# Global rows copied by VectorE alone, a planner that counts GpSimd's eight transfers, and a new order of loads, in a sliding-window attention followed by a two-layer MLP

## The chip, the cores and the metric

The kernel runs on one core of a Trainium2 chip. The metric is the device time in microseconds (us) of one execution; smaller is better. The kernel before took 221.41 us (median of 3 runs, 220.68 to 222.15). Each execution also reports the span of the core (from its first to its last instruction, some 1.8 us shorter than the time) and the mean granted clock of TensorE, where 1.0 is full speed. A run is called slow when it is over 1.5% above the fastest run of the same kernel.

## The reference, cut to what matters

```python
# q, k, v: [4 batches, 8 heads, 768 positions, 64], float32;  w_in: [512, 2048], w_out: [2048, 512]
rel = pos[:, None] - pos[None, :]
is_global = pos[None, :] < 8
is_local = (rel >= 0) & (rel < 96)
keep = is_global | is_local
scores = q @ k.T / 8 - slope[head] * dist          # dist = rel inside the window, 96 for global keys
a = softmax(where(keep, scores, -1e9))
x = (a @ v) with the heads side by side            # [3072, 512]
h = x @ w_in
out = (h - tanh(h)) @ w_out                        # [3072, 512]
```

A query tile of 128 positions needs the keys of its own tile, the last 96 positions of the tile before, and the first eight (global) positions of its batch. There are 24 tiles, numbered 0 to 23, six to a batch.

## The kernel before

The program is planned while it is being built. Every piece of work is an entry with an engine (or a choice of engines), an assumed duration, what it must come after, and the buffers that it takes and gives back. A greedy planner puts the entries in order of time, and each engine then executes its entries strictly in that order. So a wrong assumption of the planner changes no result, but it can put a piece of work behind something that waits.

For tile `u`: GpSimd issues the loads of k, q and v, which also cast float32 to bfloat16. TensorE transposes q and k (`T`; from tile `PE_T` on, a DMA transpose does it). TensorE makes scores with the own tile and with the tile before (`S`), ScalarE the exponentials (`E`), VectorE the masks (`M`), TensorE the product with v (`AV`), VectorE the division (`R`). The result is transposed into `xT` (`X` on TensorE, or a DMA transpose). Then come 16 slices of the first projection (`m1`), `h - tanh(h)` on ScalarE and VectorE, and the second projection (`m2`).

Keys of the previous tile that lie outside the window leave room, so the global keys and values are copied into its first eight rows:

```python
    def a_K(u, e):
        (nc.gpsimd if e is POOL else nc.vector).tensor_copy(out=qk[u][:, 1, :, 0:G], in_=qk[u - u % NQ][:, 1, :, 0:G])

    def a_V(u, e):
        (nc.gpsimd if e is POOL else nc.vector).tensor_copy(
            out=vb[u % NV][0:G, :, 0:Dh], in_=vb[(u - u % NQ) % NV][0:G, :, 0:Dh]
        )
    ...
        if 1 <= i < NQ - 1:
            op(("K", u), (DVE, POOL), (0.2, 0.35), lambda e, u=u: a_K(u, e), after=[("S", u, 0)])
            op(("V", u), (DVE, POOL), (0.3, 0.7), lambda e, u=u: a_V(u, e), after=[("AV", u)])
        op(("AV", u), PE, 0.5, lambda u=u: a_AV(u),
           after=[(pm, u, 0), (pm, u, 1) if i else None, ("ld", "v", u), ("V", u - 1) if i >= 2 else None],
           take=["big"], give=["p0", "p1"] if i else ["p0"])
```

So `AV` of tile u + 1 waits for the copy `V` of tile u. The planner may give a copy to VectorE or to GpSimd, whichever it thinks is done first. The loads stand in GpSimd's order too:

```python
    before = [
        ("t", 0), ("t", 1), ("t", 2), ("in", 0), ("in", 1), ("in", 2), ("t", 3), ("t", 4), ("in", 3),
        ("out", 0), ("out", 1), ("out", 2), ("out", 3), ("t", 5), ("t", 6), ("t", 7),
    ]
    ...
            op(key, POOL, us, fn, after=[prev and ("issue", prev)] + free_v, take=["kq"] if nm == "k" else [],
               dma=dma, pri=-2)
```

`("t", u)` is the k, q and v of tile u, `("in", j)` and `("out", j)` are quarters of the weights. The built program of before has nine copies on GpSimd: three of V and six of K.

The softmax here doesn't subtract the row's maximum and nothing guards it: scores larger than these inputs give would overflow.

## Time and profile before

| | before (profiled run) |
|---|---|
| time of this run / median of the timed runs | 224.73 / 221.41 us |
| span | 223.0 us |
| TensorE busy | 212.1 us, 95% |
| VectorE, ScalarE, GpSimd busy | 59%, 57%, 32% |
| longest wait of TensorE | 3.6 us, at 60 us |
| mean granted clock | 0.992 |

The profiled run is slow, 1.8% above the fastest. These are lines of the page: busy time by engine, then the span in 40 slices (a digit is the busy share in tenths), and the chain of work that ended last.

```profile
span 223.0 us, 5219 instructions
...
PE 212.1 (95%) x2130; PEld 136.7 (61%) x2130; DVE 130.7 (59%) x265; ACT 126.4 (57%) x206; POOL 70.8 (32%) x94
...
PE   7979999999859999999999999999999999999993
...
DMA  9999999999999627999999999824312111011112
...
PE 74%; DMA 18%; POOL 5%; issue 1%; ACT 0%; DVE 0%; SPq 0%; POOLq 0%
```

TensorE bounds the kernel, and its row has one hole after the start, in slices 11 and 12, near 60 us. The waits of TensorE (who waited for whom: us in total, times, longest) name it:

```profile
engine line waited for: us in total, times, longest us
PE big L235 <- POOL vb_109 L250: 3.6, 1, 3.6
PE one L291 <- DMA w_in_bf_94<-in_moe_w_in_dram: 1.4, 1, 1.4
```

Line 235 is in `a_AV`, line 250 is the V copy of tile 7 into buffer vb_109. GpSimd's own timeline (start, duration, what, and in brackets the idle time before it with its releaser) shows why the copy came late:

```profile
50.75 0.88 POOL L157 DMA_DIRECT2D vb_105<-in_v_dram  x1
...
58.34 0.88 POOL L157 DMA_DIRECT2D kq<-in_k_dram  x1 [0.18 <-PE big L235]
62.40 0.88 POOL L157 DMA_DIRECT2D kq<-in_q_dram  x1 [3.19 <-DMA vb_105<-in_v_dram]
63.27 0.60 POOL L250 COPY vb_109<-vb_108 8x512 bf16<-8x512 bf16 x1
```

The load at 62.40 had to wait for the load of vb_105, which is the eighth before it (50.75 and the seven issues up to 58.34), and the copy that TensorE needed stood behind this load. A table of stretches around the hole (columns: stretch, length, then busy time with count of PE, PEld, DVE, ACT and POOL, the granted clock, a DMA share and GB/s) shows the second part of the loss:

```profile
60.00:62.00 2.00, 0.31 (x3) 0.10 (x2) 0.69 (x1) 0.38 (x1) 0.00 (x0) 1.00 1.93 67
62.00:64.00 2.00, 0.07 (x2) 0.07 (x2) 0.00 (x0) 0.00 (x0) 1.60 (x3) 0.91 1.65 158
64.00:66.00 2.00, 2.00 (x25) 1.38 (x25) 0.00 (x0) 0.51 (x1) 0.64 (x2) 0.50 1.73 217
66.00:68.00 2.00, 2.00 (x8) 0.76 (x7) 1.42 (x3) 1.10 (x2) 0.00 (x0) 0.73 1.61 151
```

After the wait TensorE runs at half its clock until about 67 us.

### The profile page before, as it was taken

The page shows a single profiled execution, that of the slowest core. Times are in us where ns is not written, and L with a number is a line of the kernel's source. Part 1 is how long each engine was busy: PE and PEld are TensorE (multiplying, and loading weights), DVE is VectorE, ACT ScalarE, POOL GpSimd, SP SyncE. Part 2 cuts the span into 40 slices and gives each one's busy share as a digit, 9 for nine tenths or more (in the row PEclk, how much of TensorE's full clock was granted, in tenths as well). Part 3 has the DMA queues.
Part 4 walks back from the last instruction along what each step waited for, and adds up shares of the span by engine and source line. Part 5 has one row for each costly group of instructions (what it writes and reads, how often), then busy time and mean ns, then how long its engine had stood idle before and what let it go on. Part 6 is the DMA issues. An engine that isn't in the chain of part 4 may idle for free.

```text
span 223.0 us, 5219 instructions
## 1 busy us (share of the span) xinstructions
PE 212.1 (95%) x2130; PEld 136.7 (61%) x2130; DVE 130.7 (59%) x265; ACT 126.4 (57%) x206; POOL 70.8 (32%) x94
## 2 busy tenths in 40 slices
PE   7979999999859999999999999999999999999993
PEld 2548977785437858855665656565656555555553
DVE  8545896488504758855786777576755444444300
ACT  5578775676513586653785755765573444544320
POOL 8973634988440009845303930000000000000000
PEclk9999999999979999999999999999999999999999
DMA  9999999999999627999999999824312111011112
GB/s 127 145 198 171 199 214 181 165 176 167 120 167 178 118 78 81 139 126 160 181 182 130 171 138 151 160 41 103 97 20 74 47 47 47 0 50 49 47 47 94
DMA packets 106311, 26.68 MB, mean 120 GB/s; under 512 B 100528, under 2 KB 102832, under 8 KB 106288
## 3 DMA queue, kind: packets, MB, share of 16 engines
q0 software_dynamic: 75488, 13.37, 81.8%
q1 hardware_dynamic: 29760, 12.72, 31.4%
q10 hardware_dynamic: 1040, 0.26, 0.5%
q8 instruction: 16, 0.26, 0.5%
q14 instruction: 7, 0.06, 0.1%
HBM read 27.26 MB, written 6.29 MB: 150 GB/s over the span
## 4 chain that ended last, share of the span: by engine, by line
PE 74%; DMA 18%; POOL 5%; issue 1%; ACT 0%; DVE 0%; SPq 0%; POOLq 0%
PE one L318 33%; PE one L291 31%; DMA vb_105<-in_v_dram 5%; DMA w_in_bf_97<-in_moe_w_in_dram 4%; DMA w_in_bf_95<-in_moe_w_in_dram 4%; DMA qk<-kq 4%; PE big L208 4%; POOL kq L157 2%; PE big L231 2%; PE big L235 2%; PE one L330 2%; PE one L173 0%; POOL vb_102 L157 0%; POOL vb_103 L157 0%; POOL vb_104 L157 0%
## 5 line engine op out<-in xcount | busy, mean ns | idle before, releaser
L302 ACT ACTIVATE th<-one 128x384 f32<-128x384 f32 (+1 forms) x116 | 60.6, 527 | 58.0 <-PE one L291 56.9
L308 DVE TENSOR_TENSOR g<-one,th 128x384 bf16<-128x384 f32 (+1 forms) x116 | 68.5, 597 | 41.6 <-ACT th L302 38.9
L318 PEld LDWEIGHTS <-g 128*128 128x128 bf16 x368 | 33.7, 98 | 33.0 <-issue 1.3
L216 ACT ACTIVATE pd<-big 128x1024 bf16<-128x1024 f32 x24 | 24.5, 1022 | 8.0 <-PE big L208 7.8
L291 PE MATMUL one<-xT,w_in_bf_94 128*128 128x128 bf16 (+1 forms) x224 | 25.4, 258 | 1.4 <-DMA w_in_bf_94<-in_moe_w_in_dram 1.4
L291 PE MATMUL one<-xT,w_in_bf_95 128*128 128x128 bf16 (+1 forms) x224 | 25.3, 257 | 0.4 <-DMA w_in_bf_95<-in_moe_w_in_dram 0.4
L291 PE MATMUL one<-xT,w_in_bf_97 128*128 128x128 bf16 (+1 forms) x224 | 25.3, 257 | 0.1
L291 PE MATMUL one<-xT,w_in_bf_96 128*128 128x128 bf16 (+1 forms) x224 | 25.1, 257 | 0.0
L318 PE MATMUL one<-w_out_bf_101,g 128*128 128x512 bf16 x92 | 24.5, 390 | 0.0
L216 ACT ACTIVATE po<-big 128x1024 bf16<-128x1024 f32 x20 | 20.5, 1026 | 5.7 <-PE big L208 5.7
L157 POOL DMA_DIRECT2D kq<-in_q_dram x23 | 20.7, 901 | 9.3 <-DMA vb_105<-in_v_dram 3.2
L318 PE MATMUL one<-w_out_bf_100,g 128*128 128x512 bf16 x92 | 23.7, 380 | 0.0
L318 PE MATMUL one<-w_out_bf_98,g 128*128 128x512 bf16 x92 | 23.7, 380 | 0.0
L318 PE MATMUL one<-w_out_bf_99,g 128*128 128x512 bf16 x92 | 23.6, 379 | 0.0
L157 POOL DMA_DIRECT2D kq<-in_k_dram x23 | 20.6, 897 | 7.2 <-DMA kq<-in_q_dram 2.5
L291 PEld LDWEIGHTS <-w_in_bf_94 128*128 128x128 bf16 x224 | 17.6, 114 | 7.7 <-DMA w_in_bf_94<-in_moe_w_in_dram 1.5
L291 PEld LDWEIGHTS <-w_in_bf_96 128*128 128x128 bf16 x224 | 17.6, 114 | 5.7
L291 PEld LDWEIGHTS <-w_in_bf_97 128*128 128x128 bf16 x224 | 17.5, 114 | 5.9 <-DMA w_in_bf_97<-in_moe_w_in_dram 0.3
L346 ACT COPY ot<-one 128x512 f32<-128x512 f32 x23 | 13.5, 588 | 12.8 <-PE one L318 12.8
L291 PEld LDWEIGHTS <-w_in_bf_95 128*128 128x128 bf16 x224 | 17.3, 113 | 5.6 <-DMA w_in_bf_95<-in_moe_w_in_dram 0.7
L220 DVE TENSOR_TENSOR pd<-pd,mk 128x1024 bf16<-128x1024 bf16 x21 | 14.5, 690 | 7.4 <-ACT pd L216 7.3
L220 DVE TENSOR_TENSOR po<-po,mk 128x1024 bf16<-128x1024 bf16 x18 | 12.4, 691 | 10.2 <-ACT po L216 10.2
(104 smaller groups left out, 198.0 us busy)
## 6 DMA issues: line engine op xcount, KB each, us to landing
out_dram<-ot SPq DMA_DIRECT2D x23, 256.0 KB, 2.5
kq<-in_k_dram POOLq DMA_DIRECT2D x23, 128.0 KB, 10.8
kq<-in_q_dram POOLq DMA_DIRECT2D x23, 128.0 KB, 11.1
w_in_bf_94<-in_moe_w_in_dram POOLq DMA_DIRECT2D x1, 512.0 KB, 7.5
w_in_bf_95<-in_moe_w_in_dram POOLq DMA_DIRECT2D x1, 512.0 KB, 9.5
w_in_bf_96<-in_moe_w_in_dram POOLq DMA_DIRECT2D x1, 512.0 KB, 11.1
w_in_bf_97<-in_moe_w_in_dram POOLq DMA_DIRECT2D x1, 512.0 KB, 9.7
w_out_bf_98<-in_moe_w_out_dram POOLq DMA_DIRECT2D x1, 512.0 KB, 9.8
```

Source lines behind the costliest of these rows:

```text
L157: nc.gpsimd.dma_start(out=dst, in_=src.rearrange("h p d -> p h d"))
L208: nc.tensor.matmul(s[:, hh * NP + p, :], qk[u - o][r, 1, p, :], qk[u][r, 0, p, :], start=(u >= PE_B), stop=(u >= PE_B or p == NP - 1),)
L216: nc.scalar.activation(pr[u, o], s, AF.Exp, bias=0.0, scale=scale)
L220: nc.vector.tensor_tensor(out=pr[u, o], in0=pr[u, o], in1=mk[:, :, m, :], op=ALU.mult)
L231: nc.tensor.matmul(dst, pr[u, 0][:, SLOT[h], :], vb[u % NV][:, h, :], start=True, stop=last,)
L235: nc.tensor.matmul(dst, pr[u, 1][:, SLOT[h], :], vb[(u - 1) % NV][:, h, :], start=False, stop=True,)
L291: nc.tensor.matmul(t[:, (f - f0) * n : (f - f0 + 1) * n], w_in_bf[j][:, c, i : FJ * P : FJ], xT[b][:, c, o : o + n], start=(c == 0), stop= ...
L302: nc.scalar.activation(h_view(ths[g, f0], g), h_view(hs[g, f0], g), AF.Tanh, bias=0.0, scale=1.0)
L308: nc.vector.tensor_tensor(out=gs[b][:, f0 : f0 + m, o : o + n], in0=h_view(hs.pop((g, f0)), g), in1=h_view(ths.pop((g, f0)), g), op=ALU.su ...
L318: nc.tensor.matmul(os_[u], gs[u // HT][:, f, t * P : (t + 1) * P], w_out_bf[f // FJ][:, f % FJ, :], start=(f == 0), stop=(f == CF - 1),)
L330: nc.tensor.matmul(os_[u, d][:, 0:w], gs[u // HT][:, f, t * P : (t + 1) * P], w_out_bf[f // FJ][:, f % FJ, d * w : (d + 1) * w], start=(f ...
L346: nc.scalar.copy(out=ots[u], in_=os_.pop(u))
```

## The change

The intent: (1) only VectorE copies global rows, so nothing that TensorE waits for stands in GpSimd's order; (2) the planner learns that a load waits until the eighth load before it has landed; (3) loads and weights come in another order, and the planner's numbers are tuned to it: attention runs 4.5 tiles ahead of the MLP instead of 6.5, tile 9 is transposed by DMA instead of TensorE, and matmuls of zeros, meant to keep TensorE busy at the start, end at 17 us in the plan instead of 19.

```diff
-    PE_T, PE_X = 10, 5
+    PE_T, PE_X = 9, 5
...
-    def a_K(u, e):
-        (nc.gpsimd if e is POOL else nc.vector).tensor_copy(out=qk[u][:, 1, :, 0:G], in_=qk[u - u % NQ][:, 1, :, 0:G])
+    def a_K(u):
+        nc.vector.tensor_copy(out=qk[u][:, 1, :, 0:G], in_=qk[u - u % NQ][:, 1, :, 0:G])
...  (a_V in the same way)
-    AHEAD = 6.5
-    WARM = (1.3, 19.0)
-    T_LD, T_ST, T_DT, T_DX = 0.95, 0.7, 1.75, 0.9
+    AHEAD = 4.5
+    WARM = (1.3, 17.0)
+    T_LD, T_ST, T_DT, T_DX = 0.9, 0.7, 1.75, 0.9
...
-        ("t", 0), ("t", 1), ("t", 2), ("in", 0), ("in", 1), ("in", 2), ("t", 3), ("t", 4), ("in", 3),
-        ("out", 0), ("out", 1), ("out", 2), ("out", 3), ("t", 5), ("t", 6), ("t", 7),
+        ("t", 0), ("t", 1), ("t", 2), ("in", 0), ("in", 1), ("t", 3), ("in", 2), ("out", 0), ("out", 1),
+        ("in", 3), ("out", 2), ("t", 4), ("out", 3), ("t", 5), ("t", 6), ("t", 7),
...
+    ring = []
...
-            op(key, POOL, us, fn, after=[prev and ("issue", prev)] + free_v, take=["kq"] if nm == "k" else [],
+            under = [ring[-8]] if len(ring) >= 8 else []
+            op(key, POOL, us, fn, after=[prev and ("issue", prev)] + free_v + under, take=["kq"] if nm == "k" else [],
                dma=dma, pri=-2)
+            ring.append(key)
...
-            op(("K", u), (DVE, POOL), (0.2, 0.35), lambda e, u=u: a_K(u, e), after=[("S", u, 0)])
-            op(("V", u), (DVE, POOL), (0.3, 0.7), lambda e, u=u: a_V(u, e), after=[("AV", u)])
+            op(("K", u), DVE, 0.2, lambda u=u: a_K(u), after=[("S", u, 0)])
+            op(("V", u), DVE, 0.3, lambda u=u: a_V(u), after=[("AV", u)])
```

More of the change, by code (lines that the diff above doesn't have):

```diff
@@ L247, in a_R, with a_V @@
         )
-    def a_V(u, e):
-        (nc.gpsimd if e is POOL else nc.vector).tensor_copy(
+    def a_V(u):
+        nc.vector.tensor_copy(
             out=vb[u % NV][0:G, :, 0:Dh], in_=vb[(u - u % NQ) % NV][0:G, :, 0:Dh]
```

## The prediction

> **What bounds it now.** TensorE: the page has it busy 95% of a 223.0 us span, and the chain of waits is 74% TensorE. Start-to-start times in the timeline (16 first-projection matmuls 0.89 us, four second-projection 0.86, and so on) add up to about 200 us of work after 5.75 us that no order can remove. About 9 us more are start-up waits and pauses around score matmuls; about 5 us are one stall.
>
> **The stall.** In the waits, "PE big L235 <- POOL vb_109 L250" is 3.6 us, once. In the timeline GpSimd issues a kq load at 58.3, stands still until 62.40 for the load of vb_105 (issued 50.75, landed 61.8), issues the next load, and only then copies the global V rows (0.60 us at 63.27). The built order shows why: each load on GpSimd waits for the one eight before it, which the old planner did not know, and the copy stood behind such a load. After the gap the granted clock is 0.5 until about 67 us (windows): about 1.5 us more, 5.2 in all. The Trainium skill, "TensorE: Matmul & The Clock Gate" (Part 1), says that some 3.4 us of idleness halves the clock; this trace agrees.
>
> **How much is in the timed runs.** The profiled run took 224.73 us, the timed ones 220.7 to 222.2; the dip explains the profile's mean clock of 0.992. I read this as a shorter stall without the dip in timed runs: 5.2 - 3.3, about 2 us.
>
> **What the change does.**
> 1. Copies of global rows all go to VectorE. V: 0.29 us there, 0.60 to 0.78 on GpSimd; K: about 0.2 on both. Nine copies move, about 2 us more on a VectorE that is 59% busy: no cost by itself. The stall goes: -2 us (timed), -5 (profile).
> 2. The planner holds each load until the eighth before it has landed. No new wait.
> 3. New order of loads. Weights land 2.45 us apart, tiles' loads 0.85, so estimated landings are w_in 2 at 23.3 (20.6 before), w_in 3 30.6 (28.2), w_out 0 25.7 (30.7), tile 4 near 35 (25). TensorE's new order uses early w_out; walking both orders to 43 us leaves after 0 to 0.5 us ahead.
> 4. Tile 9 is transposed by DMA: -0.45 us of TensorE, one more DMA transpose.
> 5. Attention runs less far ahead. Around 58 to 70 us TensorE now wants the transposed x of tiles 5 and 6 and q/k of tile 9 while the DMA engines are still full: a new wait of 0 to 2 us is likely (+0.7).
>
> Sum: 221.4 - 2 - 0.45 - 0.3 + 0.7, less a little: the timed stall may be longer: **218.4 us**, 80% range 215.8 to 220.9. Chances: faster by over 2% 0.18, within 2% 0.78, slower 0.04.
>
> **What the profile would show.** Right: no POOL copies of qk or vb; no TensorE wait over 3 us after 20 us; granted clock 1.0 throughout, so the span falls by 4 to 6 us, more than the timed runs; GpSimd still waiting for landings, with nobody behind it; VectorE busy about 132 us. Wrong: a wait of TensorE for DMA or VectorE over 1 us at 55 to 75 us, or first projections waiting for w_in 2 or 3.
>
> **What would make me wrong.** Timed runs of before hold the whole 5 us stall: then 216. Or VectorE, strictly in order, stands before a copy that waits for a late transpose, and TensorE stalls long enough to halve its clock again: then no gain or a loss.

## The result, and the profile after

The changed kernel took 218.84 us (median of 5 runs, 218.51 to 219.75); the kernel before, in the same rounds, 221.93 us (220.68 to 225.15; the 225.15 is a slow run and not in the ratio). The ratio of the fast runs is 0.9883, 95% interval 0.9847 to 0.9919. A ratio here is that of the two kernels' fast runs as the record gives it, with its interval; it is not quite the quotient of the medians quoted, or of the means in the table below. The result is 1.2% faster, within the 2% called the same, and the prediction of 218.4 us is 0.4 us off. The profiled run of after is fast (219.75 us). The same lines of its page:

```profile
span 217.9 us, 5184 instructions
...
PE 207.3 (95%) x2095; PEld 135.5 (62%) x2122; DVE 129.5 (59%) x271; ACT 126.0 (58%) x207; POOL 67.7 (31%) x85
...
PE   7958999999999999999999999999999999999993
...
DMA  8999999999999999999995999541424121001112
...
PE 87%; DMA 5%; POOL 4%; issue 1%; DVE 1%; ACT 0%; POOLq 0%
```

The hole near 60 us is gone, and DMA's part of the chain fell from 18% to 5%. (In this trace 2,095 matmuls are recorded beside 2,122 weight loads: 27 records are missing, so the busy time is a little low. Gaps of 0.2 us put down to "issue" are these.) The waits of TensorE, and GpSimd's timeline at the same place:

```profile
engine line waited for: us in total, times, longest us
PE one L291 <- DMA w_in_bf<-in_moe_w_in_dram: 2.8, 2, 2.4
...
PE one L291 <- ACT th L302: 0.3, 1, 0.3
```

```profile
58.24 0.88 POOL L157 DMA_DIRECT2D kq<-in_q_dram  x1
59.11 0.88 POOL L157 DMA_DIRECT2D vb<-in_v_dram  x1
66.80 0.88 POOL L157 DMA_DIRECT2D kq<-in_k_dram  x1 [6.81 <-DMA qk<-kq]
```

The table of stretches at the same place, with TensorE busy and its clock at 1.00 throughout:

```profile
60.00:62.00 2.00, 2.00 (x41) 1.84 (x40) 1.69 (x5) 0.60 (x1) 0.00 (x0) 1.00 1.97 151
62.00:64.00 2.00, 1.95 (x31) 1.73 (x30) 1.97 (x5) 0.97 (x2) 0.00 (x0) 1.00 2.33 144
64.00:66.00 2.00, 2.00 (x34) 1.81 (x32) 0.82 (x2) 1.42 (x3) 0.00 (x0) 1.00 1.18 80
66.00:68.00 2.00, 2.00 (x39) 1.91 (x38) 1.57 (x3) 1.21 (x2) 1.20 (x2) 1.00 1.71 158
```

GpSimd now stands still even longer, 6.81 us, for a buffer, and no one on TensorE waits behind it. TensorE's longest wait is now at 14 us, for the first quarter of w_in: 2.4 us here, 1.4 us in the trace of before. The loads up to this weight are issued in the same order in both kernels, so this is not the change; it landed at 16.7 us here and at 15.5 us there, and it varies between executions of one program (below).

To compare traces free of this start, I took the stretch from the start of the 17th first-projection matmul (the first that needs the second quarter of w_in; in every kernel below TensorE has done the same matmuls before it, but for some of zeros) to the end of TensorE's last matmul. Both times are read from the timelines. Before: 18.32 to 219.60, so 201.3 us. After: 19.26 to 214.65, so 195.4 us. The difference is 5.9 us in these two traces, while the spans differ by 5.1.

### The profile page after: what moved, and what is told of

Read it like the earlier page. It is cut to its first block, busy times and chain, and to the rows that moved or that the text cites. A ratio compares the mean times of both kernels' runs of the same rounds, so it can differ in the third digit from the quotient of the medians.

```text
span 217.9 us, 5184 instructions
## 1 busy us (share of the span) xinstructions
PE 207.3 (95%) x2095; PEld 135.5 (62%) x2122; DVE 129.5 (59%) x271; ACT 126.0 (58%) x207; POOL 67.7 (31%) x85
## 4 chain that ended last, share of the span: by engine, by line
PE 87%; DMA 5%; POOL 4%; issue 1%; DVE 1%; ACT 0%; POOLq 0%
PE one L291 39%; PE one L318 36%; PE big L208 5%; DMA w_in_bf<-in_moe_w_in_dram 5%; PE big L231 2%; PE big L235 2%; POOL kq L157 2%; PE one L330 2%; PE one L173 1%; POOL vb L157 1%; POOL w_in_bf L161 0%; DVE x L244 0%; DVE g L308 0%; ACT th L302 0%; PE one L258 0%
## 5 line engine op out<-in xcount | busy, mean ns | idle before, releaser
L291 PE MATMUL one<-xT,w_in_bf 128*128 128x128 bf16 (+1 forms) x896 | 97.0, 258 | 3.1 <-DMA w_in_bf<-in_moe_w_in_dram 2.8
L318 PE MATMUL one<-w_out_bf,g 128*128 128x512 bf16 x342 | 87.4, 379 | 2.2 <-issue 1.3
L291 PEld LDWEIGHTS <-w_in_bf 128*128 128x128 bf16 x896 | 69.1, 114 | 26.6 <-DMA w_in_bf<-in_moe_w_in_dram 3.3
L318 PEld LDWEIGHTS <-g 128*128 128x128 bf16 x368 | 33.8, 98 | 31.8
L157 POOL DMA_DIRECT2D vb<-in_v_dram x24 | 21.9, 911 | 27.8 <-DVE rden L243 25.2
L244 DVE TENSOR_TENSOR x<-big,rden 128x512 bf16<-128x512 f32 x24 | 16.6, 692 | 0.8
L208 PE MATMUL big<-qk 64*128 64x128 bf16 x352 | 15.4, 218 | 0.0
L231 PE MATMUL big<-vb,pd 128*128 128x65 bf16 x192 | 14.0, 193 | 0.0
L231 PEld LDWEIGHTS <-pd 128*128 128x128 bf16 x192 | 12.5, 97 | 2.1 <-ACT pd L216 0.4
L235 PE MATMUL big<-vb,po 128*128 128x65 bf16 x160 | 12.4, 193 | 0.0
L235 PEld LDWEIGHTS <-po 128*128 128x128 bf16 x160 | 10.4, 97 | 1.1
```

The costliest lines, as they stand in the source:

```text
L157: nc.gpsimd.dma_start(out=dst, in_=src.rearrange("h p d -> p h d"))
L208: nc.tensor.matmul(s[:, hh * NP + p, :], qk[u - o][r, 1, p, :], qk[u][r, 0, p, :], start=(u >= PE_B), stop=(u >= PE_B or p == NP - 1),)
L231: nc.tensor.matmul(dst, pr[u, 0][:, SLOT[h], :], vb[u % NV][:, h, :], start=True, stop=last,)
L235: nc.tensor.matmul(dst, pr[u, 1][:, SLOT[h], :], vb[(u - 1) % NV][:, h, :], start=False, stop=True,)
L244: nc.vector.tensor_tensor(out=xs[u].rearrange("q (a h) d -> q a h d", a=2), in0=t[:, :, :, 0:Dh], in1=rden.to_broadcast([P, 2, H // 2, Dh] ...
L291: nc.tensor.matmul(t[:, (f - f0) * n : (f - f0 + 1) * n], w_in_bf[j][:, c, i : FJ * P : FJ], xT[b][:, c, o : o + n], start=(c == 0), stop= ...
```

## The experiments

Twelve sets of runs, of ten kernels, were taken in three groups, each group on one chip (group 1 on chip 0, groups 2 and 3 on chip 11) and with five rounds beside the kernel before. All gave correct results. "Fast mean" is the mean time of the fast runs; "stretch" is the one just defined, from the one profiled run of each.

| run | what it is | fast runs | fast mean, us | ratio to before (95%) | stretch, us |
|---|---|---|---|---|---|
| group 1: before | | 8 of 12 | 221.47 | 1 | 201.3 (first trace) |
| e1 | plan of before, all nine copies run on VectorE | 6 of 6 | 219.70 | 0.9911 (0.9856-0.9966) | 196.2 |
| e2 | plan of before, one V copy run on VectorE | 6 of 6 | 220.00 | 0.9930 (0.9880-0.9980) | 197.2 |
| e4 | after, copies allowed on GpSimd | 6 of 6 | 218.60 | 0.9867 (0.9830-0.9904) | 195.0 |
| e7 | before, new order and numbers only | 6 of 6 | 217.97 | 0.9838 (0.9804-0.9873) | 195.2 |
| group 2: before | | 9 of 11 | 221.08 | 1 | |
| a0 | after again | 6 of 6 | 218.82 | 0.9904 (0.9866-0.9943) | 194.8 |
| e3 | before, eight-transfer rule only | 6 of 6 | 220.31 | 0.9972 (0.9938-1.0005) | 196.3 |
| e5 | after, old order of loads | 5 of 6 | 219.25 | 0.9924 (0.9886-0.9962) | 195.5 |
| e6 | after, tile 9 transposed on TensorE | 6 of 6 | 220.14 | 0.9960 (0.9909-1.0011) | 196.0 |
| group 3: before | | 5 of 11 | 221.97 | 1 | |
| a1 | after, third time | 6 of 6 | 218.52 | 0.9838 (0.9783-0.9892) | 195.3 |
| e7_again | e7 again | 6 of 6 | 218.39 | 0.9832 (0.9774-0.9889) | 194.8 |
| i3 | after, six more matmuls of zeros | 6 of 6 | 218.96 | 0.9857 (0.9799-0.9916) | 195.1 |
| i1 | after, first weight before tile 2 | 6 of 6 | 220.98 | 0.9945 (0.9890-1.0000) | 196.3 |

The theory (A): the stall behind GpSimd's waiting load is most of what the change removes, and any edit that takes the copy from behind that load removes it. The rivals: (B) the gain is in the new order of loads and of TensorE's work; (C) it is half and half; (D) copies on GpSimd cost something everywhere.

### e1: the same plan, the nine copies executed by VectorE

The planner decides as before, so that the order of TensorE's instructions is the same, one for one; only the engine is swapped when the copy is emitted.

```diff
-                o["fn"] = lambda fn=o["fn"], e=e: fn(e)
+                run = DVE if key[0] in ("K", "V") else e
+                o["fn"] = lambda fn=o["fn"], e=run: fn(e)
```

> The kernel before with its plan kept (TensorE's order is the same, instruction for instruction) and only the nine copies of global rows that stood on GpSimd run on VectorE, at the same places of the program. Theory A, the stall behind GpSimd's loads is the whole loss: no TensorE wait over 1 us near 60 us, granted clock 1.0, span 217.5 to 218.5, time 218.8 to 219.8, ratio to before about 0.989, the same as the full change within 0.3%. Rival B, the gain comes from the new order of loads and of TensorE: ratio 0.997 to 1.003, span above 220. Rival C, both halves: ratio about 0.994.

Measured: 219.4 us median, ratio 0.9911, profiled span 218.3 us, clock 1.0. GpSimd still stands still for landings (idle 1.00, 1.07 and 1.58 us before these loads), and no one waits for it:

```profile
58.02 0.87 POOL L157 DMA_DIRECT2D kq<-in_q_dram  x1 [1.00 <-DMA vb<-in_v_dram]
58.88 0.90 POOL L157 DMA_DIRECT2D vb<-in_v_dram  x1
60.85 0.87 POOL L157 DMA_DIRECT2D kq<-in_k_dram  x1 [1.07 <-DMA kq<-in_q_dram]
63.30 0.88 POOL L157 DMA_DIRECT2D kq<-in_q_dram  x1 [1.58 <-DMA vb<-in_v_dram]
```

The copy of tile 7 ran on VectorE at 59.02, before TensorE used it at 60.79; its old place on GpSimd is behind the load of 63.30. The first line below is VectorE's, the others are TensorE's longest waits, of which none is near 60 us:

```profile
59.02 0.28 DVE L250 COPY vb<-vb 8x512 bf16<-8x512 bf16 x1
...
PE one L291 <- DMA w_in_bf<-in_moe_w_in_dram: 2.4, 3, 1.7
PE one L283 <- DVE vb L563: 1.2, 1, 1.2
PE one L318 <- issue: 0.8, 5, 0.2
```

So A's mechanism holds: with TensorE's order untouched, the engine of the copies alone is worth 1.8 us of fast runs (221.47 - 219.70; by the ratio's interval 0.8 to 3.2), and 5.1 us of the stretch in the traces (201.3 - 196.2), where the trace of before is of a slow run with the dip of the clock. A's "whole loss" does not: the newly planned kernels of the same group are another 1.1 us (e4) and 1.7 us (e7) faster, so e1 holds half to two thirds of the group's gain of 2.9 to 3.5 us. (All six runs of e7 are faster than all of e1; e4's overlap with them.) Of the stretch it holds 5.1 of the 5.9 to 6.5 us that the traces of the changed kernel are below before. For the remaining 0.8 to 1.4 us two terms are at hand: the eight transposes of tile 9, 0.45 us, and a wait of 0.35 us for w_in 3 at 28.9 us in e1, where no trace of the changed kernel has a wait for a weight after 20 us. That these two are the rest is argued, not shown.

### e2: a single copy

```diff
+                run = DVE if key == ("V", 7) else e
```

> As e1, but a single copy, the V copy of tile 7 that TensorE was seen to wait for, goes to VectorE; the other eight stay on GpSimd. Theory A: this one copy is the loss, so the time is that of e1 within 0.3% (218.8 to 219.8). Rival D: GpSimd's copies cost something everywhere (slower there, loads held behind copies), so one copy brings at most half of e1's gain, 220 to 221.

Measured: ratio 0.9930, 0.3 us behind e1, and no wait of TensorE near 60 us. One copy of nine brings 1.5 of e1's 1.8 us, so D is out as a main cause. The interval of the difference would also allow e2 and e1 to be equal: in its profiled run e2 lost 1.6 us at 28 us to the landing of w_in 3, which came 1.1 us later than in e1 in the same order of loads.

### e4: the changed kernel, with copies allowed on GpSimd

The diff is the reverse of the change's edits of `a_K`, `a_V`, `("K", u)` and `("V", u)`. The planner leaves the order of TensorE and ScalarE untouched, and puts three K copies and the V copy of tile 7 on GpSimd.

> The changed kernel with the copies allowed on GpSimd again; the planner, which knows the eight-transfer rule, leaves TensorE's order the same and puts one V copy (again of tile 7) and three K copies on GpSimd. In the trace of the changed kernel GpSimd does not wait for a landing before the load that now precedes that copy, so theory A expects no stall of TensorE over 1 us and 218.5 to 219.5, equal to the changed kernel within 0.3%. If copies on GpSimd are bad in themselves (rival D): 220 or more, with a TensorE wait for a POOL copy at 58 to 62 us.

Measured: ratio 0.9867, 218.6 us. The same V copy is on the same engine as before:

```profile
56.91 0.88 POOL L157 DMA_DIRECT2D kq<-in_q_dram  x1
58.38 0.77 POOL L250 COPY vb<-vb 8x512 bf16<-8x512 bf16 x1 [0.59 <-PE big L235]
59.10 0.88 POOL L157 DMA_DIRECT2D vb<-in_v_dram  x1
```

GpSimd was waiting for TensorE here, not TensorE for GpSimd. The copy takes 0.77 us instead of 0.29 on VectorE, and nobody waits for it. So the ban on GpSimd is not what the gain needs: what matters is whether the load ahead of the copy has to wait.

### e3: the eight-transfer rule alone

```diff
+            under = [ring[-8]] if len(ring) >= 8 else []
-            op(key, POOL, us, fn, after=[prev and ("issue", prev)] + free_v, ...
+            op(key, POOL, us, fn, after=[prev and ("issue", prev)] + free_v + under, ...
+            ring.append(key)
```

> The kernel before with the eight-transfer rule given to the planner and nothing else: old order of loads, copies allowed on GpSimd, where the planner again puts the V copy of tile 7, but now straight behind the last load that it believes free. If the rule alone lets the planner avoid the stall: no TensorE wait for a POOL copy over 1 us, 219 to 219.8 (as e1). If not, because a copy still stands behind loads whose landings it misjudges: a wait of 1 us or more for a POOL copy between 55 and 75 us, and 220 to 222.

Measured: no stall. The planner moved the copy of tile 7 ahead of a load of v, and it ran at 58.80:

```profile
57.93 0.88 POOL L157 DMA_DIRECT2D kq<-in_q_dram  x1 [1.06 <-DMA vb<-in_v_dram]
58.80 0.60 POOL L250 COPY vb<-vb 8x512 bf16<-8x512 bf16 x1
59.35 0.87 POOL L157 DMA_DIRECT2D vb<-in_v_dram  x1
```

The stretch is 196.3 us, as in e1, and the mean span of its fast runs is 217.93 us, 1.25 us under before's 219.18. Yet its time is only 0.3% better, with an interval that includes no gain, and lies outside the 219 to 219.8 us that I had written: time less span is 2.4 us on average here and 1.8 us for a0 on the same chip. In two of its six runs it is 1.8 us, and these took 219.7 and 219.8; in the other four it is 2.4 to 2.9. What happens in that time outside the span no view shows; it stays open. The rule also made the planner reorder TensorE's work, so this is no test at fixed order as e1 is. By the trace the rule alone removes the stall; by the timed runs its worth is not settled.

### e7: the new order and numbers alone

The kernel before with the change's `before` list, `PE_T`, `AHEAD`, `WARM` and `T_LD`, without the rule, and with the copies free to go to GpSimd.

> The kernel before with the new order of loads and the new planner numbers (PE_T 9, AHEAD 4.5, WARM 17, T_LD 0.9), but with no eight-transfer rule and with copies allowed on GpSimd. The built program has TensorE's order of the changed kernel and only two late K copies on GpSimd. Theory A: with no copy behind a waiting load there is no stall, so 218.5 to 219.5, equal to the changed kernel within 0.3%: then the order alone does what the other two parts do. If the rule or the ban is needed: above 220.5.

The built program turned out to be that of the changed kernel, instruction for instruction on TensorE, ScalarE, SyncE and in the loads, but for two K copies late on GpSimd. Measured: 217.87 us median, ratio 0.9838. That is better than the ratios of the changed kernel until then, so it was run again beside it.

> e7 again beside the changed kernel. The programs differ in two K copies late on GpSimd. If these do not matter, as I think: within 0.3% of a1 either way, and the earlier 0.3% to 0.5% were the start-up. If they do: 0.4% or more faster than a1 again.

Measured: 218.39 us against 218.52 for a1, ratios 0.9832 and 0.9838. They are equal; the earlier gap was between groups. So with the new order and numbers the planner kept all V copies, and all but two late K copies, off GpSimd without being told, and the other two parts of the change, the rule and the ban, add nothing measurable to it. They are safeguards against the next order. The numbers `AHEAD`, `WARM` and `T_LD` were not tested one by one.

### a0 and a1: the changed kernel twice more

> The changed kernel again, on the chip and in the rounds of the next three. Also a test of e7, which built to the same program but for two K copies late on GpSimd and measured 217.9 against 218.8: if that was the chip and the start-up of the day, the changed kernel gives 217.8 to 218.6 here and a ratio near 0.984 to 0.988; if the two copies matter, 218.8 or more again.

> The changed kernel once more, as the control of the next three on one chip. Its own remaining loss is the wait for the first quarter of w_in at 14 us: 1.4 to 2.6 us in the traces so far, after which one trace shows the clock at half for about 3 us. Expected 218.0 to 219.2.

Measured: 218.82 and 218.52 us, as expected for a1. a0 missed: its time is in the range that I had written for the rival, that the two copies matter, and its ratio, 0.9904, is above my 0.984 to 0.988; e7_again, above, decided against that rival. Its trace shows what varies. The first quarter of w_in landed at 16.4 us, TensorE waited 2.2 us, and then ran at half its clock:

```profile
14.12 0.20 PE L235 MATMUL big<-vb,po 128*128 128x65 bf16 x1
16.48 1.90 PE L291 MATMUL one<-xT,w_in_bf 128*128 128x128 bf16 x16 [2.16 <-DMA w_in_bf<-in_moe_w_in_dram]
18.17 1.06 PE L201 MATMUL big<-bm,ident 128*128 128x512 bf16 x2
```

The 16 matmuls took 1.90 us, against 1.08 in the trace of after, where a wait of 2.4 us at the same place was followed by full clock (why, the last section tells). The landing of this weight in the traces of one and the same program was 16.7, 16.4 and 15.3 us, and the spans of these profiled runs were 217.9, 218.1 and 216.4. So most of the spread of the changed kernel in the traces is its start.

### e5 and e6: the order of loads, and tile 9

e5 puts the old `before` list into the changed kernel; e6 sets `PE_T` to 10.

> The changed kernel with the old order of loads and weights. My account: the order of loads is worth about 0.3 us by itself, so 218.6 to 219.4, at most 0.4% over a0. Rival: early w_out is what keeps TensorE fed before 45 us, and 220 or more, with TensorE waits for w_in or w_out of over 1 us after 20 us.

> The changed kernel with tile 9 transposed on TensorE as before. I costed the move to DMA at 0.45 us of TensorE time, eight transposes of 56 ns: so 0.3 to 0.6 us over a0 (0.15% to 0.3%), if TensorE is never short of work around there. If the DMA transposition cost as much in waiting: within 0.1% of a0.

Measured: e5 219.25 us, 0.4 us (0.2%) over a0, and 195.5 us of stretch against a0's 194.8, with waits of 0.7 and 0.5 us for copies of q/k and xT after 20 us, none for weights. That is the expected size, and within the noise; the traces of the changed kernel themselves have stretches of 194.8 to 195.4. e6 is 220.14 us, 1.3 us over a0: over twice the expected 0.3 to 0.6. Its profiled run and one more had a clock near 0.990, dipping at the start as in a0, which is part of it; its stretch is 196.0 us, 0.6 to 1.2 more than the three traces of the changed kernel. Of that 0.35 us is the dip, which still lasted when the stretch began: its first 32 matmuls took 2.33 us, against 1.98 in after. Of the 1.3 us of time 0.36 lies outside the span (time less span is 2.15 us here, 1.79 for a0). Eight transposes of 56 ns are 0.45 us of what is left. The rest is not explained, since the planner reorders other work with it, and the intervals of a0 and e6 overlap.

### i1 and i3: what is left at the start

i1 loads the first quarter of w_in before tile 2; i3 puts six more matmuls of zeros before the first matmul that needs it.

```diff
-        ("t", 0), ("t", 1), ("t", 2), ("in", 0), ("in", 1), ("t", 3), ("in", 2), ("out", 0), ("out", 1),   # i1
+        ("t", 0), ("t", 1), ("in", 0), ("t", 2), ("in", 1), ("t", 3), ("in", 2), ("out", 0), ("out", 1),
...
+        at = next(t for t, key in order if key == ("m1", 0, 0))                                            # i3
+        for n in range(n, n + 6):
+            ops["warm", n] = dict(eng=PE, us=0.22, fn=warm)
+            order.append((at - 0.001, ("warm", n)))
```

> The changed kernel with the first quarter of w_in loaded before tile 2 and planned anew. If the order of these loads sets the start: the first quarter lands near 12.5 us, TensorE's idle time before 20 us falls by 1 us or more, and the time is 217 to 218. If the DMA engines just move the same hole (tile 2 comes 2.5 us later): within 0.3% of a1, with a wait of TensorE for tile 2 or for w_in 1 in its place.

> The changed kernel with six more matmuls of zeros (about 1.3 us at full clock) just before the first one that needs w_in, where TensorE was seen idle for 1.4 to 2.6 us. They cost nothing as long as w_in lands later than that. If the dips of the clock after this wait are a cost of the timed runs: no clock under 0.997 in any run, and 0.2 to 0.5 us off the mean of the changed kernel, with a smaller spread. If the dips are rare or harmless: within 0.1% of a1. If the hole is at times shorter than 1.3 us: slower by up to 0.5 us.

i1: the weight landed at 12.9 us as expected, and the wait for it shrank. But tile 2 came later, seven matmuls of zeros filled the next hole, attention fell behind, and TensorE waited for VectorE later (twice, around 50 us):

```profile
PE big L208 <- DVE x L244: 1.2, 2, 0.8
...
PE one L291 <- DMA w_in_bf<-in_moe_w_in_dram: 1.1, 2, 0.7
PE one L173 <- DMA kq<-in_q_dram: 0.4, 1, 0.4
```

Its mean span is 218.23 us against a1's 216.75, and 1.0 us more of its time lies outside the span: worse than both outcomes that I had written. The hole moved and grew. i3: no clock under 0.998, but 218.96 us against 218.52, no gain; two of the six runs of i3 were at or under a1's mean. The dips cost too little, or come too seldom, for filling to show. No version beats the changed kernel clearly; e7 equals it.

## Why the prediction was right or wrong, point by point

The time (218.4 predicted, 218.84 measured) and the class (within 2%) were right. Step by step:

- **The stall, -2 us in timed runs and -5 in the profile: right.** e1 isolates it: -1.8 us of fast runs and -5.1 us of stretch. The step that took the profile's 5.2 us down to 2 rested on the profiled run being 3.3 us over the median, with a clock of 0.992. In the three groups 18 of the 22 fast runs of before show a clock of 0.997 or more. But no trace of a fast run of before exists, so that its stall is shorter there is inferred from e1's gain, not seen. e1's trace, of a fast run, rather speaks for a long one: the copy's old place is behind a load that ended at 64.18, 3.4 us after TensorE used the copy. So the size in timed runs may be right by luck.
- **The rule adds no wait: right**, and e3's trace shows that it alone lets the planner avoid the stall. That was more than I had credited it with: I had credited the end of the stall to the ban on GpSimd alone. e4 and e7 show that the ban is not needed.
- **Order of loads, -0.3 us: not contradicted, and not shown** (e5: 0.4 us, within noise). The estimated landings were 23.3, 30.6 and 25.7 us for w_in 2, w_in 3 and w_out 0; the trace has 24.3, 31.8 and 26.8, all about 1.1 us late, as the first weight was.
- **Tile 9 by DMA, -0.45 us: not contradicted.** e6 measured 1.3 us over a0, six runs against six, with a spread that reaches down to the estimate; the traces say 0.6 to 1.2, or 0.3 to 0.9 without the 0.35 us of the dip.
- **A new wait of 0.7 us at 58 to 70 us: wrong.** After 24 us no wait of TensorE in the trace of after reaches 0.4 us. The transposes issued between 51 and 68 us did take 6.7 to 11.5 us from issue to landing, but TensorE did not wait for them.
- **Clock 1.0 throughout: not quite.** The wait for the first weight at the start is still there, and in some runs it halves the clock (a0).
- **VectorE busy about 132 us: 129.5 measured.** The copies are short, and other work of VectorE measured a little less; this did not matter.

The total was right in part because two errors met. The terms as written add up to 219.35; I took off 0.95 more for a timed stall longer than 2 us, which e1's mean does not show (its interval does not exclude it), and had added 0.7 for a wait that did not come. Without these two the sum is 218.65, beside 218.84 measured.

The Trainium skill says, in "TensorE: Matmul & The Clock Gate" under "Architectural detail", that GpSimd is strictly first in, first out on each of its cores. The trace agrees, for the order of the queue: the V copy, which had to come after the products of tile 7 (the last began at 57.92 us), ran at 63.27, straight after the load that could not issue until 62.40. In "DMA: Bandwidth & Descriptors", "Issuing engines are not separate DMA queues", it says that transfers issued by different engines run on the same 16 DMA engines and interleave. The trace agrees in that packets of GpSimd's queue and of SyncE's, which has the stores and the transposes, move in the same stretch (1,973 and 84 from 51 to 53 us); that they share engines is the page's word. The load of vb_105, issued at 50.75 while transposes were under way, landed at 61.83, 11.1 us later, where the first four loads took 4.4 to 4.8 us. The transposes need not be the reason: before any transpose by DMA, behind three quarters of w_in, the loads issued at 10.2 to 12.0 us took 11.2 to 11.3 us.

Of the runs of before in the three groups 12 of 34 were slow; of the changed kernel's three sets (18 runs) none, of e1 and e2 (12 runs) none. All but two of these 12 had a clock between 0.983 and 0.992; one had 1.0, and one, of 360 us, had 0.561. The stall may be what makes most of them slow; as only slow runs show it, it is not claimed here.

## What to carry to other kernels

Don't put work that the bounding engine waits for behind a queue entry that can block: a copy of 0.6 us on a mostly idle engine cost 5 us in a trace, and about 2 in the timed runs, because a load ahead of it was waiting for an older load to land. When one plan decides everything, test the parts of a change at fixed order (e1) and by themselves (e3, e7) before crediting one of them: here any of three edits removed the stall in the traces. And compare stretches that begin after a noisy start, or the start will be taken for an effect.

## What the Trainium skill lacked or had wrong

- "TensorE: Matmul & The Clock Gate", Part 1, gives an idle window of about 3.4 us before the clock is halved, and "Why this matters for your kernels" advises no idle gaps over about 3 us. Here a wait of 2.2 us (2.4 us from matmul to matmul) was enough in one run (a0: clock 0.51 from 16.4 to 18 us), and one of 1.8 us in e6, while a wait of 2.4 us in another run of a0's program was followed by full clock. A free-running window, as that page describes it, fits the difference, but the stated length is no safe limit. The traces show the window: clock changes lie on a grid of 3.41 us (half from 16.44 to 19.86 in a0, from 63.65 to 67.06 in before). A step of the grid with 2.12 us (a0, 13.03 to 16.44) or 1.81 us (e6, 13.27 to 16.68) of TensorE idle was followed by half clock; the wait of 2.4 us in after fell into two steps, with 1.68 and 1.21 us idle, and e1 had 1.71 us in one step, both without a dip. So in these traces the limit lay between 1.71 and 1.81 us of idle time per step, about half of it.
- No page read names the limit of eight loads. In the built program and the trace a load waited for the landing of the eighth before it: 3.19 us at 59.2 us, until vb_105 landed at 61.83. It is a wait of the program: the packed trace has the loads report their landing on eight semaphores in turn (104 to 111), and the load at 62.40 waits on 105, the one of vb_105. How many loads the hardware would take, no run shows.
- "DMA: Bandwidth & Descriptors" gives no figure for how long loads take beside DMA transposes; here loads of 128 KB took 4.4 to 4.8 us from issue to landing at the start, 11.1 us at 50.75 us with transposes in flight, and 11.2 to 11.3 us at 10.2 to 12.0 us behind weights, without any.
